# Moving the sums of v from GpSimd (four operations a group) to VectorE (three), with new slots around them

## The chip, the cores and the metric

The kernel runs on one core of a Trainium2 chip. The metric is the device time of one execution in microseconds (us); a "time" below is the median of several executions. All runs used here are fast: there is one core, and no run was more than 1.5% above the fastest of its kernel.

## The reference, cut to what matters

```python
def _attn_ref(u, v, z):                      # u, v: 8 x 3008 x 256, z: 8 x 3008 x 64
    scores = scale * np.matmul(z, z.transpose(0, 2, 1))
    attn = np.maximum(scores, 0.0) ** 2      # a, symmetric, 3008 x 3008 for each batch
    out = np.matmul(attn, v)
    return u * out

def _moe_ref(x, w_in, w_out):                # x: all 24064 rows of the above
    h = x @ w_in                             # 256 -> 2048
    g = h * np.cos(h)
    return g @ w_out                         # 2048 -> 256
```

## The kernel before

There are 8 batches. A batch is worked off in 6 column groups of 512 rows. TensorE makes scores, ScalarE takes their relu, VectorE squares them to `a`, TensorE multiplies `a` by `v`; at the same time, and in the same instruction streams, TensorE multiplies by `w_in`, ScalarE takes the cosine, VectorE makes the product `g`, and TensorE multiplies `g` by `w_out`.

The author places every piece by hand on a time axis of "slots": 8 for a column group, 48 for a batch, about 3.3 us each (in the trace before, on average 158 us from one change of batch to the next, divided by 48). Events are sorted by slot and issued in that order, so a number in these tables fixes a piece's place in its engine's order.

For some blocks `a.v` is done with seven products in place of eight. This needs sums (differences, here) of blocks of v and of blocks of a. The sums of v, four for each of four groups `R` in a batch, are made by GpSimd:

```python
    TSUM = [-2.0, -1.9, -0.8, 2.0, 2.5]     # slots of the sums of v, for each group R
    ...
    def v_sums(b, R):
        j = R * K
        t = vs(b, j // G)
        k1, k2 = (slice(j % G + 2 * i, j % G + 2 * i + 2) for i in range(2))
        d1, d2 = slice(0, P), slice(P, 2 * P)
        o = vsum[R]
        after(nc.gpsimd.tensor_tensor(o[:, 0], t[:, k1, d2], t[:, k1, d1],
                                      ALU.subtract).ins, before[-1], NOSYNC)
        nc.gpsimd.tensor_tensor(o[:, 2], t[:, k2, d2], t[:, k1, d2], ALU.subtract)
        nc.gpsimd.tensor_tensor(o[:, 1], t[:, k2, d2], o[:, 0], ALU.subtract)
        nc.gpsimd.tensor_tensor(o[:, 3], t[:, k2, d1], o[:, 1], ALU.subtract)
    ...
        for R in range(NW):
            at(b * span + (TSUM[R] if b else 2 * U + R), 2, lambda b=b, R=R: v_sums(b, R))
```

`NOSYNC` fixes an order and makes no wait. Groups 0 and 1 stand at slots -2.0 and -1.9, just before the change of batch at slot 0.

The first sums of a are VectorE operations with both inputs in SBUF; the product `g` is a VectorE operation with one input in PSUM (here PSUM holds what TensorE writes, SBUF all other tiles):

```python
    def a_sums1(b, c, R):
        s1 = quarters(b, c, R, (0, 1))
        after(nc.vector.tensor_tensor(s1, s1, quarters(b, c, R, (1, 1)), ALU.add).ins,  # line 422
              before[-1], NOSYNC)
        nc.vector.tensor_tensor(                                                        # line 424
            second(b, c, R), s1, quarters(b, c, R, (0, 0)), ALU.subtract)
    ...
    def h_quantum(m, ft):
        ...                                  # two matmuls into hp, a PSUM tile of a pool of six
        nc.scalar.activation(c16, hp, AF.Sin, bias=math.pi / 2.0, scale=inv_s2)
        ...
        nc.vector.tensor_tensor(gs[(m, ft // FG)][:, ft % FG, :], hp, c16, ALU.mult)    # line 506
```

The score matmuls take their PSUM tiles from the same pool of six. So TensorE gets on only when `g` products and relus free them.

In the views below, PE stands for TensorE (PEld for its weight loads), DVE for VectorE, ACT for ScalarE, POOL for GpSimd. "Half clock" means that the trace's clock records grant TensorE 0.5 of its full clock.

Of the kernel before, what the change touches and what calls it, by code (L numbers as in the profile page):

```python
# [14 lines left out]
def kernel(  # L15
# [9 lines left out]
    nc = tc.nc  # L25
    AF = mybir.ActivationFunctionType
    ALU = mybir.AluOpType
# [5 lines left out]
    P = 128  # L33
# [6 lines left out]
    K = CW // P  # L40
    NC = NJ // K
    G = 8
# [5 lines left out]
    NSLOT = 18  # L48
    NW = 4
    PLAN = {  # L50
        0: [(1.0, 'P1 P5 P2'), (2.35, 'B1'), (2.55, 'P6 B1'), (3.0, 'P7 B1'),
            (3.4, 'P3'), (4.55, 'A1'), (5.0, 'P4 A1'), (5.4, 'B1'), (6.15, 'B3'),
            (6.35, 'B2'), (6.55, 'A2'), (7.0, 'A2 B2'), (7.4, 'A5')],
        1: [(1.0, 'P1 P5 P2'), (2.15, 'P6'), (3.0, 'P7 B1'), (3.4, 'P3'), (4.15, 'B1'),
            (4.35, 'B1'), (4.55, 'B1'), (4.75, 'P4 A1'), (5.0, 'A1 B1'), (5.4, 'B2'),
            (6.35, 'A1'), (6.55, 'B1'), (6.75, 'A3'), (7.0, 'A1 B1'), (7.4, 'A4 B2')],
        2: [(0.75, 'P1 P2'), (1.0, 'P5'), (1.4, 'P6'), (2.15, 'B1'), (2.75, 'B1'),
            (3.0, 'P7 P3 B1'), (4.75, 'P4 B1'), (5.0, 'A1 B1'), (5.4, 'A1 B1'),
            (6.15, 'A1 B1'), (6.35, 'A1'), (6.75, 'A1'), (7.0, 'A1 B3'), (7.4, 'A5 B1')],
        3: [(1.0, 'P1 P5 P2'), (2.15, 'P6 B1'), (2.55, 'B1'), (2.75, 'B2'), (3.0, 'P7'),  # L60
            (3.4, 'P3'), (4.55, 'A1 B1'), (5.0, 'P4 A1 B2'), (5.4, 'A1 B1'),
            (6.15, 'A1'), (6.55, 'A2'), (6.75, 'B1'), (7.0, 'A2 B1'), (7.4, 'A3 B1')],
        4: [(0.75, 'P1 P5'), (1.0, 'P2'), (2.15, 'P6'), (3.0, 'P7'), (3.4, 'P3 A1'),
            (4.35, 'B1'), (4.75, 'P4 A1 B1'), (5.4, 'B1'), (6.15, 'B1'), (6.35, 'A1 B1'),
            (6.55, 'B1'), (6.75, 'A1 B1'), (7.4, 'A3')],
        5: [(1.0, 'P1 P5'), (1.4, 'P2'), (2.15, 'P6'), (2.55, 'B2'), (3.0, 'P3'),
            (3.4, 'P7'), (4.35, 'B1'), (4.75, 'P4 A1'), (5.4, 'A1 B2'), (6.15, 'A2'),
            (6.35, 'A1'), (7.0, 'A2 B1'), (7.4, 'B1')],
    }
    SUM1, SUM2, WADD, RADD = {0: (-3.9, 0.65), 1: (-3.8, 0.35), 2: (-2.4, 0.3), 3: (-2.9, 0.7), 4: (-3.65, 0.55), 5: (-3.0, 0.75)}, {0: (1.95, 0.02), 1: (1.85, 0.02), 2: (1.95, 0.02), 3: (1.6, 0.02), 4: (2.0, 0.02), 5: (1.85, 0.02)}, {0: 5.26, 1: 4.96, 2: 4.26, 3: 4.36, 4: 4.26, 5: 4.46}, {0: 4.45, 1: 5.75, 2: 4.15, 3: 4.05, 4: 3.55, 5: 4.65}  # L70
    TSUM = [-2.0, -1.9, -0.8, 2.0, 2.5]
    XEND = 4.0
    WSET = {0: [0, 1, 2], 1: [0, 1, 2], 2: [0, 1, 2], 3: [0, 1, 2], 4: [0, 1, 2, 3], 5: [0, 1, 2, 3]}
    HALF = {0: 5.2, 1: 3.9, 2: 3.7, 3: 4.1, 4: 4.2, 5: 4.7}

    inv_s = 1.0 / float(S)
    inv_s2 = inv_s * inv_s
# [13 lines left out]
    vs = lambda b, g: vring[(b * NG + g) % (NG + 1)]  # L91
# [7 lines left out]
    before = []  # L99
    NOSYNC, SYNC = mybir.DependencyClass.NoSync, mybir.DependencyClass.Sync  # L100

    def after(ins, other, cls):
        tc.add_manual_dep(
            ins, other.name,
            mybir.DependencyInfo(cls, mybir.DependencyReason.DATA), reason="order")
# [126 lines left out]
    def direct(b, c, R):  # L232


        return b == 0 and c <= 2
# [148 lines left out]
    def v_sums(b, R):  # L384

        j = R * K
        t = vs(b, j // G)
        k1, k2 = (slice(j % G + 2 * i, j % G + 2 * i + 2) for i in range(2))
        d1, d2 = slice(0, P), slice(P, 2 * P)
        o = vsum[R]  # L390
        after(nc.gpsimd.tensor_tensor(o[:, 0], t[:, k1, d2], t[:, k1, d1],
                                      ALU.subtract).ins, before[-1], NOSYNC)
        nc.gpsimd.tensor_tensor(o[:, 2], t[:, k2, d2], t[:, k1, d2], ALU.subtract)
        nc.gpsimd.tensor_tensor(o[:, 1], t[:, k2, d2], o[:, 0], ALU.subtract)
        nc.gpsimd.tensor_tensor(o[:, 3], t[:, k2, d1], o[:, 1], ALU.subtract)

    def by_key(b, c, R):
        return R < c or triangle(b, c, R)
# [136 lines left out]
    def at(t, rank, f):  # L535
        events.append((t, rank, len(events), f))
# [11 lines left out]
    for b in range(B):  # L548
        pairs = [(b, c, R, p) for c, R in groups for p in range(2)]
        for i in range(0, len(pairs), NV):  # L550
            some = [pr for pr in pairs[i:i + NV] if not direct(*pr[:3])]
            t = b * span - lead + span * i / len(pairs)
# [32 lines left out]
    for b in range(B):  # L585
        for R in range(NW):
            at(b * span + (TSUM[R] if b else 2 * U + R), 2, lambda b=b, R=R: v_sums(b, R))
        for c in range(NC):
            t = b * span + c * U
            W = seven(b, c)  # L590
            d = direct(b, c, c)
            ready = 1.5 + when[(b, c, NC - 1)]
            first, last = (0.6, 6.93) if d else (HALF[c] if W else 1.0, 7.3)
            room = [i for i, sc in enumerate(scores)
# [59 lines left out]
    for m in range(NT):  # L654
        b, i = divmod((m + 1) * TW - 1, S)
# [7 lines left out]
    for b in range(B):  # L663
        t = b * span
# [73 lines left out]
```

## Time and profile before

| | before |
|---|---|
| time, median of 4 (range) | 1266.78 us (1265.1 to 1270.8) |
| span of the profiled run | 1266.8 us |
| TensorE busy / idle (from its first to its last matmul) | 1229.4 / 33.1 us |
| granted clock of TensorE, mean | 0.98 |
| VectorE, ScalarE, GpSimd busy | 1057.0, 836.1, 237.8 us |

From the page of the profile before: the busy time of each engine, and the granted clock in 40 slices of the span, in tenths (9 is 90% or more).

```profile
PE 1229.4 (97%) x8439; PEld 774.7 (61%) x8439; DVE 1057.0 (83%) x1977; ACT 836.1 (66%) x1744; POOL 237.8 (19%) x329
...
PEclk9999899998999989999999998999989999899999
```

TensorE looks full. But the clock row has six 8s, evenly spaced but for one missing in the middle: each lies at a change of batch (the 8 at the fifth slice covers 127 to 158 us, the next 285 to 317 us, and so on); the change to batch 4, in the slice from 601 to 633 us, has the shortest stretch of half clock and still rounds to 9. The same from the windows of before, a steady stretch and the first change of batch: the stretch, its length, busy time of each engine, then clock, DMA share and GB/s.

```profile
140.00:290.00 150.00, 149.67 (x1046) 96.17 (x1046) 124.78 (x247) 103.12 (x218) 19.86 (x28) 0.98 0.70 114
129.00:146.00 17.00, 12.10 (x58) 5.79 (x57) 15.49 (x19) 8.63 (x19) 13.22 (x20) 0.80 1.09 130
```

In the steady stretch TensorE is busy for 149.67 of 150 us (the first 6 us of it still belong to the change, hence the clock of 0.98). In the 17 us of the change it does 58 matmuls; at the steady rate (1046 in 150 us) it would do 119.

The waits of TensorE, before (who waited for whom: us in total, times, longest):

```profile
PE w L263 <- DVE g L506: 26.3, 19, 4.4
PE acc L351 <- DVE x L380: 2.5, 1, 2.5
```

The score matmul (line 263) waits for `g` products to free PSUM. VectorE's groups, before (count, busy us and mean ns of one, idle time before):

```profile
L506 DVE TENSOR_TENSOR g<-w,c 128x512 f16<-128x512 f32 x752 | 490.7, 683 | 55.9 <-ACT c L503 53.9
L301 DVE TENSOR_TENSOR s<-rt 128x1024 f16<-128x1024 f16 x254 | 180.4, 717 | 102.3 <-ACT rt L299 101.1
L424 DVE TENSOR_TENSOR s<-s 128x512 f16<-128x512 f16 x119 | 83.3, 705 | 1.5
L422 DVE TENSOR_TENSOR s<-s 128x512 f16<-128x512 f16 x119 | 51.4, 437 | 0.0
```

Lines 424 and 422 have the same size and type, yet one has a mean of 705 ns and the other of 437. A mean hides the cause; the timeline shows it. The first change of batch, before (start, duration, instruction, in brackets idle time before it and what ended it):

```profile
131.24 6.36 DVE L424 TENSOR_TENSOR s<-s 128x512 f16<-128x512 f16 x1
...
131.65 1.31 POOL L391 TENSOR_TENSOR vsum<-v 128x256 f16<-128x256 f16 x2
...
132.91 1.29 POOL L394 TENSOR_TENSOR vsum<-v,vsum 128x256 f16<-128x256 f16 x2
...
134.16 1.28 POOL L395 TENSOR_TENSOR vsum<-v,vsum 128x256 f16<-128x256 f16 x2
134.50 0.39 PE L263 MATMUL w<-zT 64*128 64x512 f16 x1
135.41 1.28 POOL L393 TENSOR_TENSOR vsum<-v 128x256 f16<-128x256 f16 x2
136.66 0.66 POOL L391 TENSOR_TENSOR vsum<-v 128x256 f16<-128x256 f16 x1
137.40 0.73 POOL L394 TENSOR_TENSOR vsum<-v,vsum 128x256 f16<-128x256 f16 x1
137.53 1.15 DVE L301 TENSOR_TENSOR s<-rt 128x1024 f16<-128x1024 f16 x1
...
139.33 0.86 PE L263 MATMUL w<-zT 64*128 64x384 f16 x2 [4.44 <-DVE g L506]
139.37 0.60 ACT L503 ACTIVATE c<-w 128x512 f16<-128x512 f32 x1 [6.12 <-DVE g L506]
```

One VectorE operation, which takes 0.42 us elsewhere, lasts 6.36 us, while GpSimd makes nine sums without a gap; it ends at 137.60, just after that run. TensorE meanwhile has an idle block of 4.44 us. The changes to batches 2 and 3 show the same. In those to batches 4 to 7 the operation lasts 4.50 us, over six sums, and TensorE's longest idle block is 2.1 to 2.6 us. Over the whole trace, the VectorE operations that are more than 0.1 us above the median of their form exceed it by 49.5 us, 49.1 us of this in 45 operations that overlap a GpSimd sum, all with two inputs in SBUF. The 70 with an input in PSUM that overlap a sum exceed it by 0.01 us at most.

After each block the trace's clock records give TensorE half its clock, for 3.4 to 10.2 us, 47.8 us in the seven changes of batch.

### The profile page before, as it was taken

The numbers are of one execution on the slowest core, as the hardware profiler recorded it, in microseconds if no ns is written. First come the engines' busy times: TensorE is split into PE (matmuls) and PEld (weight loads), VectorE is DVE, ScalarE is ACT, GpSimd is POOL, SyncE is SP. The second block draws the span as 40 slices with busy tenths as digits, with TensorE's granted clock in tenths as the row PEclk, the third lists the DMA queues.
The fourth block names the chain that finished last, engine by engine and source line by source line (L and its number), as shares of the span: only waits on it lengthen the run. The fifth ranks groups of instructions, "written<-read, shape, count | busy, mean of one in ns | idle before, by whom it ended". The sixth has DMA issues, their size and how long they took to land.

```text
span 1266.8 us, 23106 instructions
## 1 busy us (share of the span) xinstructions
PE 1229.4 (97%) x8439; PEld 774.7 (61%) x8439; DVE 1057.0 (83%) x1977; ACT 836.1 (66%) x1744; POOL 237.8 (19%) x329
## 2 busy tenths in 40 slices
PE   8999899998999989999999999999999999999999
PEld 3366466664666656666566665666656666566666
DVE  8888878888788887888878888788887888878875
ACT  6667577675776757767676676676766767667655
POOL 4611401014010140101401014010140101400000
PEclk9999899998999989999999998999989999899999
DMA  9997758677687786868868678786796756966401
GB/s 159 171 160 117 108 106 122 118 123 106 107 119 122 123 107 107 119 121 123 116 104 124 118 115 122 103 126 111 115 133 103 124 108 109 139 106 101 85 26 51
DMA packets 484226, 145.02 MB, mean 114 GB/s; under 512 B 432400, under 2 KB 484112, under 8 KB 484112
## 3 DMA queue, kind: packets, MB, share of 16 engines
q1 hardware_dynamic: 356448, 88.73, 43.4%
q0 software_dynamic: 100400, 29.77, 23.7%
q10 hardware_dynamic: 27264, 25.06, 6.1%
q8 instruction: 66, 1.08, 0.4%
q14 instruction: 48, 0.39, 0.1%
HBM read 60.29 MB, written 24.64 MB: 67 GB/s over the span
## 4 chain that ended last, share of the span: by engine, by line
PE 90%; DVE 7%; ACT 1%; issue 1%; DMA 1%; DVEq 0%
PE w L516 25%; PE w L499 25%; PE acc L465 18%; PE acc L351 15%; PE w L263 6%; DVE s L424 3%; DVE g L506 1%; DVE s L301 1%; DMA ut<-ust 1%; ACT rt L299 1%; PE acc L328 1%; DVE s L422 0%; PE w L695 0%; ACT zT L224 0%; DVE x L380 0%
## 5 line engine op out<-in xcount | busy, mean ns | idle before, releaser
L503 ACT ACTIVATE c<-w 128x512 f16<-128x512 f32 x752 | 439.9, 616 | 286.9 <-PE w L499 197.5
L506 DVE TENSOR_TENSOR g<-w,c 128x512 f16<-128x512 f32 x752 | 490.7, 683 | 55.9 <-ACT c L503 53.9
L516 PE MATMUL w<-w_out,g 128*128 128x256 f16 x3008 | 454.9, 275 | 0.0
L499 PE MATMUL w<-x,w_in 128*128 128x512 f16 x1504 | 453.9, 385 | 0.0
L516 PEld LDWEIGHTS <-g 128*128 128x128 f16 x3008 | 297.5, 99 | 197.9 <-issue 9.3
L299 ACT ACTIVATE rt<-w 128x512 f16<-128x512 f32 x489 | 253.1, 613 | 58.1 <-PE w L263 58.1
L351 PE MATMUL acc<-s,v 128*128 128x512 f16 (+1 forms) x1000 | 284.9, 381 | 2.5 <-DVE x L380 2.5
L301 DVE TENSOR_TENSOR s<-rt 128x1024 f16<-128x1024 f16 x254 | 180.4, 717 | 102.3 <-ACT rt L299 101.1
L499 PEld LDWEIGHTS <-w_in 128*128 128x128 f16 x1504 | 148.7, 99 | 69.2 <-issue 3.1
L119 POOL DMA_DIRECT2D ust<-in_u_dram x112 | 81.6, 736 | 568.7 <-PE acc L351 549.4
L465 PE MATMUL acc<-s,vsum 128*128 128x256 f16 (+1 forms) x1208 | 157.9, 270 | 0.9 <-DVE q L481 0.5
L351 PEld LDWEIGHTS <-v 128*128 128x128 f16 x1000 | 93.2, 98 | 86.8 <-issue 37.3
L263 PE MATMUL w<-zT 64*128 64x512 f16 (+3 forms) x684 | 101.0, 367 | 29.7 <-DVE g L506 26.3
L465 PEld LDWEIGHTS <-vsum 128*128 128x128 f16 x1208 | 117.2, 98 | 17.9 <-issue 4.4
L465 PE MATMUL acc<-s,v 128*128 128x256 f16 (+1 forms) x906 | 117.6, 270 | 0.0
L434 DVE TENSOR_TENSOR s<-s,s 128x1024 f16<-128x1024 f16 (+1 forms) x151 | 95.0, 671 | 9.3 <-PE acc L465 8.9
L465 PEld LDWEIGHTS <-v 128*128 128x128 f16 x906 | 85.4, 98 | 20.4 <-issue 12.4
L424 DVE TENSOR_TENSOR s<-s 128x512 f16<-128x512 f16 (+1 forms) x151 | 95.6, 638 | 2.0
L263 PEld LDWEIGHTS <-zT 64*128 64x128 f16 x684 | 26.3, 94 | 87.3 <-issue 73.4
L523 ACT ACTIVATE ob<-w 128x256 f32<-128x256 f32 x188 | 71.1, 378 | 8.0 <-PE w L516 8.0
L380 DVE TENSOR_TENSOR x<-acc,ut 128x64 f16<-128x64 f32 (+7 forms) x178 | 68.9, 429 | 4.1 <-DMA ut<-ust 2.3
L280 ACT ACTIVATE rt<-w 128x512 f16<-128x512 f32 (+3 forms) x176 | 62.8, 449 | 11.5 <-PE w L263 8.3
(38 smaller groups left out, 443.7 us busy)
## 6 DMA issues: line engine op xcount, KB each, us to landing
out_dram<-ob ACTq DMA_DIRECT2D x92, 256.0 KB, 2.2
ust<-in_u_dram POOLq DMA_DIRECT2D x80, 128.0 KB, 4.6
v<-in_v_dram POOLq DMA_DIRECT2D x16, 512.0 KB, 6.5
s<-s SPq DMA_TRANSPOSE x249, 4.4
v<-in_v_dram POOLq DMA_DIRECT2D x8, 448.0 KB, 8.9
zst<-in_z_dram POOLq DMA_DIRECT2D x14, 128.0 KB, 4.9
ust<-in_u_dram POOLq DMA_DIRECT2D x16, 96.0 KB, 4.2
w_in<-in_moe_w_in_dram POOLq DMA_DIRECT2D x4, 256.0 KB, 10.5
```

Source lines behind the costliest of these rows:

```text
L119: hold(nc.gpsimd.dma_start(dst, src))
L263: chain(nc.tensor.matmul(sp[:, s0 * P:], zt[h, R * K + k + 1 - lo, :], zt[h, j0 + s0:j0 + K, :].rearrange("p j w -> p (j w)"), start=True, ...
L299: nc.scalar.activation(rt[:, i, :], banks[k], AF.Relu)
L301: nc.vector.tensor_tensor(t.rearrange("p s k w -> p k s w")[:, 2 * p:2 * p + 2], rv, rv, ALU.mult)
L351: chain(nc.tensor.matmul(acc[:, 0:wn], vs(b, j // G)[:, j % G, nh * P:(nh + 1) * P], a, start=(start and n == 0), stop=(last and n == len( ...
L424: nc.vector.tensor_tensor(second(b, c, R), s1, quarters(b, c, R, (0, 0)), ALU.subtract)
L434: after(nc.vector.tensor_tensor(dst, src, sub, ALU.subtract).ins, before[-1], NOSYNC)
L465: chain(nc.tensor.matmul(acc[bank][:, cols], lhs[:, k, :], rhs[:, k, :] if old else rhs[:, :, k * P:(k + 1) * P], start=(n in (1, 5) and i ...
L499: chain(nc.tensor.matmul(hp, w_in16[:, k, ft * P:(ft + 1) * P], x[:, k, :], start=(k == 0), stop=(k == NDH - 1)))
L503: nc.scalar.activation(c16, hp, AF.Sin, bias=math.pi / 2.0, scale=inv_s2)
L506: nc.vector.tensor_tensor(gs[(m, ft // FG)][:, ft % FG, :], hp, c16, ALU.mult)
L516: chain(nc.tensor.matmul(ys[m][:, 0:D], gs[(m, f4)][:, ft % FG, ts * P:(ts + 1) * P], w_out16[:, ft, :], start=(ft == 0), stop=(ft == NFT ...
```

## The change

The intent is to free GpSimd and to use VectorE's spare time: three operations in place of four (the first makes two of the four results at once), with new slots for the sums and, around them, for the pieces of `a.v`.

```diff
-    SUM1, ... = {0: (-3.9, 0.65), 1: (-3.8, 0.35), 2: (-2.4, 0.3), ...}, ...
-    TSUM = [-2.0, -1.9, -0.8, 2.0, 2.5]
+    SUM1, ... = {0: (-3.9, 0.5), 1: (-1.8, 0.4), 2: (-1.9, 0.15), ...}, ...
+    TSUM = [-2.9, -0.9, -0.8, 3.5, 3.5]
 ...  (SUM2, WADD, RADD, HALF and the table PLAN get new numbers too: cut)
     def v_sums(b, R):
 
         j = R * K
-        t = vs(b, j // G)
-        k1, k2 = (slice(j % G + 2 * i, j % G + 2 * i + 2) for i in range(2))
-        d1, d2 = slice(0, P), slice(P, 2 * P)
+        t = vs(b, j // G)[:, j % G:j % G + K, :].rearrange("p (h k) d -> p h k d", h=2)
         o = vsum[R]
-        after(nc.gpsimd.tensor_tensor(o[:, 0], t[:, k1, d2], t[:, k1, d1],
-                                      ALU.subtract).ins, before[-1], NOSYNC)
-        nc.gpsimd.tensor_tensor(o[:, 2], t[:, k2, d2], t[:, k1, d2], ALU.subtract)
-        nc.gpsimd.tensor_tensor(o[:, 1], t[:, k2, d2], o[:, 0], ALU.subtract)
-        nc.gpsimd.tensor_tensor(o[:, 3], t[:, k2, d1], o[:, 1], ALU.subtract)
+        b12, b22 = t[:, :, :, P:2 * P], t[:, 1, :, P:2 * P]
+        left = t[:, 0, :, :].rearrange("p k (d w) -> p d k w", w=P)
+        after(nc.vector.tensor_tensor(o[:, 0:3:2], b12, left, ALU.subtract).ins,
+              before[-1], NOSYNC)
+        nc.vector.tensor_tensor(o[:, 1], b22, o[:, 0], ALU.subtract)
+        nc.vector.tensor_tensor(o[:, 3], t[:, 1, :, 0:P], o[:, 1], ALU.subtract)
```

`SUM1` holds, for each column group, the slot of the first sums of a and the spacing of its three or four pairs.

## The prediction

> **What bounds the kernel now.** TensorE: 97% of the 1266.8 us span by the busy table, and 149.7 of 150 us in a steady stretch (140 to 290 us, windows), with VectorE at 83% there. Its idle time is 33 us, and the timeline shows it in few places: at each of the seven changes of batch idle blocks of 2.1 to 4.4 us with small ones behind them, 25.8 us together; the rest in the first 75 us.
>
> **Why it idles there.** At each change of batch GpSimd runs six v sums back to back, and one VectorE operation (second difference of a, 128x512, both inputs in SBUF), normally 0.42 us, takes 6.36 us in batches 1 to 3 and 4.50 us in 4 to 7: it ends when the GpSimd run ends. Operations with two SBUF inputs are longer when they overlap a sum (squares of 128x1024: 1.02 against 0.69 us); those with an input in PSUM are not (g product: 0.68 both ways). This agrees with the Trainium skill, "GPSIMD Engine Reference", section 8: contention with VectorE instructions with two SBUF inputs. VectorE then frees no PSUM buffer, and TensorE's score matmul waits for the g product: 26.3 us in the table of waits.
>
> **The second cost.** After each block the granted clock is 0.5 for 3.4 to 10.2 us (clock records; 47.8 us in the seven changes); pairs of w_in matmuls then take 1.06 instead of 0.59 us. Without the part in idle time (about 5 us) this costs (47.8 - 5) / 2 = 21 us. The skill's "TensorE: Matmul & The Clock Gate" tells of such a gate after about 3.4 us of idling; here blocks of 2.1 us were enough.
>
> **What the change does.** It removes 128 GpSimd sums (93 us busy), hence VectorE's excess of 49 us (durations above the median of their form). It adds 96 VectorE operations: 32 of 128x512 (0.42 us, as other operations of that form) and 64 of 128x256 (0.29 us): 1.0 us a group, 32 us in all. TensorE's and ScalarE's counts stay. Other pieces move by fractions of a slot; steadily busy TensorE has nothing to win there.
>
> **On the critical path.** Removed: 25.8 + 21 = 47 us, and about 2 us at the start. Given back: in each change of batch the sums of groups 1 and 2 stand together in VectorE's order (2 us), just after a v load that takes 6.5 us to land; VectorE may wait for it up to 1 us and TensorE may see part: 0 to 1.5 us a batch without a new drop of the clock, about 5 us in all. Elsewhere VectorE's spare 17% takes the 32 us.
>
> **Prediction:** 1268 - 47 - 2 + 5 = 1224 us, range 1212 to 1243. Faster by over 2%: 0.88; within 2%: 0.11; slower: 0.01.
>
> **What would show it.** The second difference at 0.42 us everywhere; TensorE's wait for the g product near zero; clock 1.0 after 50 us except at the end; VectorE busy about 1057 - 49 + 32 = 1040 us, GpSimd about 145; TensorE idle under 12 us. The block of 2.5 us at 42 us, which waits for a DMA transpose of u, stays with its half clock.
>
> **What would make it wrong.** VectorE waiting in order for the v load, or for TensorE's last use of a sum's buffer, over 2 us, which brings idle blocks and half clock back: 1240 to 1250. Sums costing much more than 0.42 + 2 x 0.29 us for their strided reading. Or the half clock having another cause: then only 26 us go, to 1242.

## The result, and the profile after

| | before | after |
|---|---|---|
| time, median of 4 | 1266.78 us | 1219.2 us (1218.26 to 1219.85) |
| ratio, 95% interval | | 0.9619 (0.9593 to 0.9646) |
| span of the profiled run | 1266.8 us | 1216.4 us |
| TensorE busy / idle | 1229.4 / 33.1 us | 1205.9 / 6.2 us |
| half clock, 50 us to the end of the matmuls | 47.8 us | 0 |

A ratio here, and in all that follows, is the mean time of one kernel's fast runs over the mean of the other's in the same rounds, so it is not quite the ratio of the medians.

The page after, its windows (the same steady stretch, and the first change of batch), and TensorE's waits. The changed file is one line longer further down, so line 506 is now 507, and 424 is 425; lines above `v_sums` moved by two (263 is 265, 301 is 303, 351 is 353).

```profile
PE 1205.9 (99%) x8439; PEld 767.9 (63%) x8439; DVE 1028.0 (85%) x2073; ACT 833.1 (68%) x1744; POOL 146.0 (12%) x201
...
PEclk9999999999999999999999999999999999999999
```

```profile
140.00:290.00 150.00, 150.00 (x1065) 96.93 (x1063) 128.40 (x264) 104.84 (x222) 17.91 (x24) 1.00 0.78 122
127.00:144.00 17.00, 17.00 (x121) 10.65 (x119) 16.40 (x37) 12.77 (x27) 4.34 (x6) 1.00 1.21 161
```

```profile
PE acc L353 <- DVE x L382: 2.2, 1, 2.2
...
PE w L265 <- DVE g L507: 0.8, 2, 0.6
```

VectorE's groups after, the old ones and the three new ones (393, 395, 396):

```profile
L507 DVE TENSOR_TENSOR g<-w,c 128x512 f16<-128x512 f32 x752 | 492.3, 683 | 60.2 <-ACT c L504 57.4
L303 DVE TENSOR_TENSOR s<-rt 128x1024 f16<-128x1024 f16 x254 | 172.7, 688 | 85.4 <-ACT rt L301 84.4
...
L425 DVE TENSOR_TENSOR s<-s 128x512 f16<-128x512 f16 x119 | 49.1, 418 | 1.7
L423 DVE TENSOR_TENSOR s<-s 128x512 f16<-128x512 f16 x119 | 48.6, 414 | 0.4 <-DMA s<-s 0.4
...
L393 DVE TENSOR_TENSOR vsum<-v 128x512 f16<-128x512 f16 x32 | 12.7, 416 | 0.0
...
L395 DVE TENSOR_TENSOR vsum<-v,vsum 128x256 f16<-128x256 f16 x32 | 8.5, 282 | 0.0
L396 DVE TENSOR_TENSOR vsum<-v,vsum 128x256 f16<-128x256 f16 x32 | 8.4, 281 | 0.0
```

The change of batch now holds 121 matmuls in 17 us, the steady rate. Line 425 is back at 418 ns. VectorE has 29.6 us more to do (12.7 + 8.5 + 8.4) and is busy 29 us less.

The span fell by 50.4 us: TensorE's idle time by 26.9 us, its busy time by 23.5 us with the same 8439 matmuls. The second part is the half clock: at half clock matmuls count as busy for longer (a pair of `w_in` matmuls takes 1.06 us there, 0.59 elsewhere in the trace before).

### The profile page after: what moved, and what is told of

It reads as the page before. It is cut to its first block, busy times and chain, and to the rows that moved or that the text cites. A ratio compares the mean times of both kernels' runs of the same rounds, so it can differ in the third digit from the quotient of the medians.

```text
span 1216.4 us, 23077 instructions
## 1 busy us (share of the span) xinstructions
PE 1205.9 (99%) x8439; PEld 767.9 (63%) x8439; DVE 1028.0 (85%) x2073; ACT 833.1 (68%) x1744; POOL 146.0 (12%) x201
## 4 chain that ended last, share of the span: by engine, by line
PE 96%; DMA 2%; DVE 1%; issue 0%; ACT 0%; DVEq 0%; ACTq 0%
PE w L517 27%; PE w L500 26%; PE acc L466 19%; PE acc L353 17%; PE w L265 6%; DMA s<-s 1%; PE acc L330 1%; DMA ut<-ust 1%; DMA v<-in_v_dram 1%; DVE s L303 0%; DVE g L507 0%; PE w L696 0%; DVE x L382 0%; DVE s L435 0%; ACT rt L301 0%
## 5 line engine op out<-in xcount | busy, mean ns | idle before, releaser
L517 PE MATMUL w<-w_out,g 128*128 128x256 f16 x3008 | 448.8, 273 | 0.0
L500 PE MATMUL w<-x,w_in 128*128 128x512 f16 x1504 | 446.0, 379 | 0.0
L517 PEld LDWEIGHTS <-g 128*128 128x128 f16 x3008 | 294.0, 98 | 191.3
L303 DVE TENSOR_TENSOR s<-rt 128x1024 f16<-128x1024 f16 x254 | 172.7, 688 | 85.4 <-ACT rt L301 84.4
L265 PE MATMUL w<-zT 64*128 64x512 f16 (+3 forms) x684 | 91.0, 361 | 2.9 <-ACT zT L226 1.1
L121 POOL DMA_DIRECT2D v<-in_v_dram x40 | 31.3, 788 | 298.3 <-PE acc L466 144.1
L425 DVE TENSOR_TENSOR s<-s 128x512 f16<-128x512 f16 (+1 forms) x151 | 61.2, 411 | 2.0
```

Source lines behind the costliest of these rows:

```text
L121: hold(nc.gpsimd.dma_start(dst, src))
L265: chain(nc.tensor.matmul(sp[:, s0 * P:], zt[h, R * K + k + 1 - lo, :], zt[h, j0 + s0:j0 + K, :].rearrange("p j w -> p (j w)"), start=True, ...
L303: nc.vector.tensor_tensor(t.rearrange("p s k w -> p k s w")[:, 2 * p:2 * p + 2], rv, rv, ALU.mult)
L500: chain(nc.tensor.matmul(hp, w_in16[:, k, ft * P:(ft + 1) * P], x[:, k, :], start=(k == 0), stop=(k == NDH - 1)))
L517: chain(nc.tensor.matmul(ys[m][:, 0:D], gs[(m, f4)][:, ft % FG, ts * P:(ts + 1) * P], w_out16[:, ft, :], start=(ft == 0), stop=(ft == NFT ...
```

## The experiments

The profile says how the old kernel lost time. It does not say which part of the change cured it, since the change does two things: another engine, and other slots. Theory H: a run of GpSimd sums holds up VectorE's operations with two SBUF inputs, then TensorE idles, then its clock is halved; moving the sums off GpSimd cures it. Rival P: the new placement makes the gain. All ratios are to the kernel before, in the same rounds.

### One half of the change at a time (e1, e2)

The old placement, the sums by VectorE:

```diff
  (kernel before, all tables unchanged)
-  v_sums as before (GpSimd, four operations)
+  v_sums as after (VectorE, three operations)
```

> The kernel before with all its placement constants, only the v sums done by VectorE in three operations. Theory H (a run of GpSimd sums holds up VectorE's operations with two SBUF inputs, TensorE idles, and its clock is halved afterwards): nearly the whole gain, 1216 to 1230 us, no half clock after 50 us. Rival P (the new placement of the pieces makes the gain): 1255 to 1268 us.

The new placement, the sums by GpSimd:

```diff
  (kernel after, all tables unchanged)
-  v_sums as after (VectorE, three operations)
+  v_sums as before (GpSimd, four operations)
```

> The changed kernel with its new placement, but the sums by GpSimd in four operations as before. H: 1255 to 1275 us, with a VectorE operation of 4 us or more and a half clock at each change of batch. P: 1219 to 1230 us.

| ratio (median time) | old placement | new placement |
|---|---|---|
| sums by GpSimd | 1 (1268.44 us) | e2: 0.9624 (1220.83 us) |
| sums by VectorE | e1: 0.9682 (1228.45 us) | after: 0.9619 (1219.2 us, other rounds) |

Each theory is right in one run and wrong in the other: e1 falls in H's range (1216 to 1230), e2 in P's (1219 to 1230). Either half takes away nearly everything, and the second half then adds 0.6% (placement, sums already on VectorE) or nothing that these runs can tell (engine, new placement already there: 0.9624 and 0.9619, with intervals that overlap). H as stated missed e2: GpSimd sums are there, 128 of them, and the longest VectorE operation is 1.31 us, with no half clock before the end.

VectorE still pays in e2: its operations with two SBUF inputs exceed their medians by 31 us where they overlap a sum, in some 80 small pieces. TensorE, with its six PSUM tiles, hardly notices pieces of half a microsecond: its longest idle block after 50 us is 0.97 us.

### Three operations on GpSimd (e3)

```diff
  (kernel after; v_sums in its new form)
-        nc.vector.tensor_tensor(...)      # three times
+        nc.gpsimd.tensor_tensor(...)
```

> The changed kernel, the same three operations, but on GpSimd. H: GpSimd needs about as long for three operations on the same 1024 elements as for four (2.4 to 2.7 us a group), so the stalls stay: 1250 to 1275 us. A rival that puts the gain down to three operations instead of four, or to the form of the operations: 1219 to 1235 us.

Measured: 1248.86 us, ratio 0.9845 (0.9827 to 0.9863). The rival (form and number of operations) falls; H's range is missed by 1 us at its lower end. Stalls of up to 3.0 us stay in the changes of batch, and there are two half clocks among the seven. At the same placement the four shorter operations of e2 took 1220.83 us: on GpSimd fewer and longer sums were worse, with a VectorE excess of 57 us against 31.

### The sums spread out on GpSimd (e4)

```diff
  (kernel after; sums by GpSimd, v_sums(b, R, i) makes the i-th of the four)
-        after(... .ins, before[-1], NOSYNC)              # the first of four
+        after(... .ins, before[-1], SYNC)                # each one: waits for a TensorE point
-            at(b * span + (TSUM[R] if b else 2 * U + R), 2, ...)
+            for i in range(4):
+                o = ([-8, -4.8, -0.9, 3][R] + [0.8, 0.8, 0.5, 1][R] * i if b
+                     else 2 * U + 2 * R + 0.5 * i)
+                at(b * span + o, 2, lambda b=b, R=R, i=i: v_sums(b, R, i))
  (and two sets of vsum, one for odd and one for even batches)
```

> The changed kernel, the sums by GpSimd in four operations, but each of them held to its own TensorE point, half a slot or more (1.6 us) from the next, with a second set of sum buffers so that they may start early. H: a stall lasts one operation (under 1 us), TensorE does not idle, no half clock after 50 us: 1218 to 1232 us. A rival in which GpSimd's sums cost VectorE in proportion to their busy time, however placed: 1245 us or more.

Measured: 1228.3 us, ratio 0.9684 (0.967 to 0.9699), longest VectorE operation 1.41 us; one half clock after 50 us, at 63 us, none in a change of batch. The excess of VectorE with GpSimd sums is 31.0 us, against 49.1 before: so GpSimd's busy time is not the price. What counts is how long VectorE is kept out at a stretch.

### Adding a wait (e11)

In e2 and e3 GpSimd operations that need the previous one's result start 0.08 us after its end; in the long runs of before they follow each other with no gap, since the scheduler issues the operations of groups 0 and 1, which are neighbours, in turns and each result is ready when needed. Theory H2: VectorE gets in at a gap, and is kept out while there is none. That asks for an odd experiment, the kernel before with a wait more:

```diff
  (kernel before; for each of the four sums, in the same places)
+            if sums:
+                after(ins, sums.pop(), SYNC)    # wait until the sum before has completed
+            sums.append(ins)
```

> The kernel before, unchanged in placement, engine and operations, but each GpSimd sum waits for the one before it to complete. Theory H2 (what costs is an unbroken run: GpSimd operations that follow each other with no gap keep VectorE's operations with two SBUF inputs out until the run ends; where GpSimd has to wait for its own result, 0.08 us here, VectorE gets in): 1220 to 1240 us, no VectorE operation over 2 us, although a wait was added. Rival G (GpSimd's busy time, or sums at this place of the batch, whatever the gaps): 1255 to 1270 us.

Measured: 1235.03 us, ratio 0.974 (0.9718 to 0.9761). One more wait in the source, and 2.6% less time. The wait changed the order too: GpSimd now makes the four sums of one group after those of the other, not in turns. From e11's timeline of GpSimd and of VectorE, the change to batch 4:

```profile
589.63 1.49 POOL L120 DMA_DIRECT2D ust<-in_u_dram  x2
591.13 1.51 POOL L395 TENSOR_TENSOR vsum<-v 128x256 f16<-128x256 f16 x2
592.72 1.75 POOL L395 TENSOR_TENSOR vsum<-v,vsum 128x256 f16<-128x256 f16 x2
```

```profile
590.71 1.40 DVE L429 TENSOR_TENSOR s<-s 128x512 f16<-128x512 f16 x1
592.03 1.15 DVE L302 TENSOR_TENSOR s<-rt 128x1024 f16<-128x1024 f16 x1
```

The same VectorE operation (line 429 here, the old 424) that took 4.50 us at this place ends after 1.40 us: it is kept out over one sum, and gets in at the gap behind it. The load in front does not hold it: in the trace after, 260 VectorE operations with two SBUF inputs overlap loads issued by GpSimd and no sum, and none exceeds its median by more than 0.01 us. Two sums with the gap between them take 1.51 us, in place of 1.31.

Counting this in seven traces (before, e2, e3, e4, e11, e12, e13): take each VectorE operation with at least 0.15 us of excess, and each end of a GpSimd sum while it waits. At some 230 ends with a gap of 0.06 us or more the VectorE operation got in, without exception; at about 160 of them the gap was under 0.15 us with another sum behind it. At ends with no gap and another sum behind them it got in some 80 times and was kept out some 70 times, 44 of these before the change. (The exact counts depend on how close to its own end an operation still counts as waiting.)

### Only the slots of the v sums, and the counterpart (e12, e13)

```diff
  (e12: kernel before)
-    TSUM = [-2.0, -1.9, -0.8, 2.0, 2.5]
+    TSUM = [-2.9, -0.9, -0.8, 3.5, 3.5]
```

> The kernel before with one line changed: the times of the sums, which are those of the changed kernel; the sums stay on GpSimd. H2: the sums of groups 0 and 1 no longer stand interleaved, the run at the bad place is broken: 1219 to 1235 us. Rival P2 (the new placement of the a.v blocks made the run with GpSimd sums and new placement fast): 1255 to 1270 us.

```diff
  (e13: kernel after with the sums by GpSimd, as e2)
-    TSUM = [-2.9, -0.9, -0.8, 3.5, 3.5]
+    TSUM = [-2.0, -1.9, -0.8, 2.0, 2.5]
```

> The counterpart: the changed kernel's whole placement, sums on GpSimd, but at the old times. H2: the unbroken run is back: 1250 to 1272 us, a VectorE operation of 4 us and half clock at each change of batch. P2: 1219 to 1228 us.

Measured: e12 1230.37 us, ratio 0.9712 (0.9686 to 0.9737): one line of slots, with all sums on GpSimd, is worth 2.9%. Group 0 no longer has group 1 as neighbour, so its sums wait for each other. But groups 1 and 2 are neighbours now, and in e12 as in e2 every change of batch has a run of five sums without a gap (3.4 to 3.8 us). VectorE's operations at that place, with an input in PSUM and with two in SBUF mixed, get in between these sums, and none lasts over 1.04 us. So e12 does not show that every run without gaps costs.

But e13 measured 1224.98 us, ratio 0.9669 (0.9647 to 0.9692), where H2 expected 1250 or more. The run of sums without gaps is there (588.5 to 594.8 us in the change to batch 4, nine sums). VectorE's squares got in twice behind its first sums, then VectorE's next four operations in order are `g` products, 589.8 to 592.3 us, which read PSUM and are not held up; only after them is a square kept out, for 2.3 us. So the run alone is not enough. Theory H3: it takes the run, and a VectorE operation with two SBUF inputs that is caught at the start of it while the `g` products stand behind.

### Two attempts to steer the coincidence (e15, e16)

```diff
  (e15: kernel before; e16: kernel e13, the reverse)
-    SUM1 ... = {0: (-3.9, 0.65), ...
+    SUM1 ... = {0: (-3.9, 0.5), ...
```

> The kernel before with one number changed: the spacing of the first sums of a in column group 0 is 0.5 slots as in the changed kernel, not 0.65, so that the third pair stands 0.3 slots (1 us) earlier in VectorE's order. All v sums stay on GpSimd at their old places. Theory H3 (it takes a coincidence: an unbroken GpSimd run, and a VectorE operation with two SBUF inputs waiting when it starts; when VectorE's next operations read PSUM instead, the run passes unnoticed): 1222 to 1238 us, no VectorE operation over 3 us. Rival H2 as stated before (the unbroken run alone suffices): 1255 to 1270 us.

> The changed kernel's placement with the sums on GpSimd, with two things put back: the old times of the v sums (alone 1225 us) and the old spacing of the first sums of a in column group 0. H3: the coincidence is whole again, a VectorE operation of 3 to 6 us in each change of batch, the half clock is back: 1250 to 1272 us. Rival P3 (the rest of the new placement makes it robust): 1222 to 1232 us.

Both missed H3's numbers. e15 measured 1253.38 us, ratio 0.9896 (0.9861 to 0.9931), between the two expectations. The operation of line 424 is no longer caught; in batches 1 to 4 the next one in order, a square of line 301, also with two SBUF inputs, is caught instead (6.3, 6.3, 6.3 and 4.4 us), and in batches 5 to 7 none is caught at that place (the longest is 2.6 us, later on). e16 measured 1225.91 us, ratio 0.9678 (0.9649 to 0.9708): the old spacing does not bring the stall back; VectorE and GpSimd take turns over the first sums.

That different batches of one execution, with the same instructions, go different ways fits a coincidence. What decides it at an end without a gap is open: in e15 the square began to wait 0.09 us before the first sum both in batch 4 and in batch 5; it was kept out over six sums in the one (4.4 us) and let in after one in the other (1.4 us).

### Reads against writes (e17, e18)

These settle the cause without any sums on GpSimd. The kernel is e1 (old placement, sums by VectorE), with six GpSimd operations added in each change of batch at slot -2.0. Their results are never used; the output stays correct.

```diff
+    def extra():
+        for i in range(6):
+            o = nc.gpsimd.tensor_tensor(junk[i][:, 0:256], src[:, 0], src[:, 1], ALU.subtract)  # e17
+            o = nc.gpsimd.memset(junk[i], 0.0)                      # e18 instead, 128x768
+            after(o.ins, before[-1], NOSYNC)
+    for b in range(1, B):
+        at(b * span - 2.0, 2, extra)
```

> The kernel with the old placement and the sums on VectorE (1228 us), to which six GpSimd subtractions of 128x256 from SBUF to SBUF, whose results nobody uses, are added in each change of batch where GpSimd's sums stood before. H3: they stop VectorE as the sums did: an operation of 4 us or more, half clock, 1255 to 1278 us. Rival D (it was the sums as data: TensorE waited for their results or for buffers): 1226 to 1234 us.

> The same, but the six GpSimd operations only write (memsets of 128x768, meant to last as long). H3: only GpSimd operations that read SBUF stop VectorE's operations with two SBUF inputs: 1226 to 1234 us, no VectorE operation over 2 us. Rival W (any unbroken GpSimd work at this place does it, for instance because it delays the loads in GpSimd's queue): as with the six reads, 1255 to 1278 us.

Measured: e17 1268.38 us, ratio 1.0019 (0.9982 to 1.0056): the whole loss is back, with all sums on VectorE. e18 1227.83 us, ratio 0.9695 (0.9665 to 0.9724): as e1. The change to batch 4 in e17's timeline:

```profile
603.27 4.50 DVE L431 TENSOR_TENSOR s<-s 128x512 f16<-128x512 f16 x1
...
603.69 3.80 POOL L401 TENSOR_TENSOR junk<-src 128x256 f16<-128x256 f16 x6
...
609.03 0.32 PE L265 MATMUL w<-zT 64*128 64x384 f16 x1 [2.12 <-DVE g L513]
```

and in e18's:

```profile
586.16 0.42 DVE L431 TENSOR_TENSOR s<-s 128x512 f16<-128x512 f16 x1
586.53 0.69 DVE L303 TENSOR_TENSOR s<-rt 128x1024 f16<-128x1024 f16 x1
586.55 4.16 POOL L401 MEMSET junk<- 128x768 f16 x6
587.14 0.68 DVE L513 TENSOR_TENSOR g<-w,c 128x512 f16<-128x512 f32 x1
587.74 0.75 DVE L393 TENSOR_TENSOR vsum<-v 128x512 f16<-128x512 f16 x2
```

GpSimd's six writes take longer than the six reads (4.16 against 3.80 us) and sit in the same queue in front of the same loads of v. VectorE passes through them at its usual pace: over the whole trace 56 operations with two SBUF inputs overlap such a write, and none exceeds its median by more than 0.01 us. So the loss is neither GpSimd's being busy, nor delayed loads, nor the sums as data. It is GpSimd reading SBUF while VectorE wants a second SBUF input. The Trainium skill says so in "SBUF — State Buffer", section "Who interferes with whom": such a VectorE instruction contends with a GpSimd instruction that reads SBUF, "not with one that only writes it". The runs agree.

### The last idle block (e14)

After the change one idle block of 2.2 us is left at 41 us, where VectorE waits for a transpose of u by DMA, with 3.4 us of half clock behind it in the profiled run.

```diff
  (kernel after)
-            at(t + c * U + (1 if b or c not in (1, 2) else -3 * c), 0, ... turn_u(b, c))
+            at(t + c * U + (1 if b or c not in (1, 2) else (-5.2, -6)[c - 1]), 0, ... turn_u(b, c))
```

> The changed kernel with the one large idle block that it has left taken away: TensorE waits 2.2 us at 41 us because the transpose of u for column group 1 stands behind a transpose of s in the DMA queue; here it is issued before the transposes of s. Theory I (an idle block of 2 us brings 3.4 us of half clock, whatever caused the block): both go, 2.2 + 1.7 = 3.9 us less than the changed kernel: 1213 to 1217 us, and the clock records show no half clock between 10 us and the end. Rival: the half clock at 42 us has another cause and stays, 1216 to 1219 us. The transposes of s that are now later could cost some of it at 25 to 60 us.

Measured: 1223.46 us, ratio 0.9663 (0.9635 to 0.9691): no gain. The block at 41 us and its half clock went, but the transposes of s are later, and at 60 us VectorE waits 4.5 us for one; TensorE gets blocks of 3.0 and 1.6 us there and 10.2 us of half clock. The wait moved down the DMA queue, and the half clock moved with it. No run was faster than the changed kernel; e2 is as fast within the noise.

### Idle blocks and the half clock, over all traces

All 14 traces together, from 20 us on: idle blocks of TensorE (over 0.15 us; those within 4 us of each other taken as one), and whether a half clock begins about them. Of 30 whose longest block is 1.7 us or more, 27 have one. Of 129 with a longest block up to 1.5 us, 4 have one. Half clocks follow blocks of every cause here: stalls by sums, by useless reads, by DMA transposes. What decides the exceptions is open.

## Why the prediction was right, and where it was not

- **The bound, right.** TensorE's idle time at the changes of batch (25.8 us) and its half clock there are gone; the profiled span fell by 50.4 us.
- **VectorE held up by GpSimd's sums, right in kind.** e17 brings the loss back with six reads and e18 does not with six writes. The sentence "it removes 128 GpSimd sums, hence VectorE's excess of 49 us" holds, but the excess as such was not what cost: e2 and e4 keep 31 us of it and still have most of the gain (0.9624 and 0.9684). And "it ends when the GpSimd run ends" is not so in the changes to batches 5 and 7, where the run goes on.
- **The half clock as a second cost, right.** Estimated 21 us; busy time fell by 23.5 us. (The trace has 8 us of idle time within the seven half clocks where the prediction took 5, so its own sum should have said 20.)
- **VectorE's price, right.** Predicted 1.0 us a group, measured 0.416 + 0.282 + 0.281 = 0.98 us. VectorE's busy time came out at 1028 us, 12 below the forecast; the sums explain 2.4 of that. The rest is how busy time is counted: the durations of all VectorE operations added up fell by 19.4 us, as 49.5 less 29.6 says, but neighbouring operations overlap a little in the profile, busy time counts an overlap once, and these overlaps grew by 9.5 us.
- **"Given back: about 5 us", wrong in size.** TensorE has no idle block over 0.15 us in any change of batch after, so this term measured nothing. VectorE did not wait for the load of v. With it at zero the sum would have been 1219 us. That this is the measured 1219.2 is partly luck: the base of 1268 is 1.2 us above the measured 1266.8, the half clock was worth 2.5 us more than estimated, and the 2 us at the start did not show as such (TensorE's idle time in the first 75 us went from 7.2 to 6.2 us).
- **"Other pieces move by fractions of a slot; steadily busy TensorE has nothing to win there", wrong.** The number did not suffer, because the two halves of the change do the same thing and do not add up. But the placement alone gains 3.8% (e2), and one line of it 2.9% (e12). The prediction looked for a gain where TensorE was full, and missed that slots also decide which GpSimd operations become neighbours, hence whether a run has gaps, and which VectorE operation meets it.

So the shown cause is: runs of GpSimd reads of SBUF in the change of batch, without gaps, catch a VectorE operation with two SBUF inputs for 4 to 6 us; TensorE runs out of PSUM tiles; its clock is halved for a while. What remains open is what lets VectorE in, or not, at an end without a gap. Open too is how the operation comes to be caught: in all seven changes of before and of e17 it had begun 0.40 to 0.43 us before the first sum or read, which is its whole usual length (0.42 us). GpSimd's times in these profiles are rough, so this may be no more than the edge of the record.

## What to carry to other kernels

When an operation's mean is far above that of another of the same size, look at the longest ones in the timeline and at what the other engine was doing; here seven operations of 119 held 34 of the 49 us by which VectorE's operations ran over their usual length. GpSimd reads of SBUF beside VectorE work with two SBUF inputs are cheap in small pieces and can be costly in a run without gaps: break the run (other slots, a wait, other order), or move it. A short idle block of TensorE costs more than its length if a half clock follows, and undoing two parts of a change one at a time is needed before either is given the credit.

## What the Trainium skill lacked or had wrong

- "SBUF — State Buffer", section "SBUF: two separate sides": the shared pair is held "for the whole instruction". The page does not say that VectorE can be kept out over many GpSimd instructions: 6.36 us over nine sums (before), 4.50 us over six reads (e17). Nor that a gap of about 0.08 us between GpSimd instructions lets VectorE in (about 160 gaps under 0.15 us, no exception), which e11 turned into 2.6%.
- "TensorE: Matmul & The Clock Gate", "Why this matters for your kernels": it advises against idle gaps of more than about 3 us. Here 20 of 23 groups of idle blocks whose longest was 1.8 to 3.0 us already had the half clock about them, and 7 of the 10 among these that were a single block (2.05 to 2.89 us).
- "GPSIMD Engine Reference", section 4.1, advises VectorE for elementwise work as GpSimd is about half as fast for two inputs. The traces show 2.3 times (0.66 us undisturbed against 0.28 us for a sum of 128x256), but here GpSimd with a fitting placement (e2, 0.9624) was as good as VectorE (0.9619).
